# Attention's weighted sums in float32 column tiles, in a kernel of attention, experts and a dense block

## The chip, the cores and the metric

The kernel runs on one core of a Trainium2 chip. The metric is device time of one execution in microseconds (us), the median of several executions. Five engines work side by side, each through its own queue in order: TensorE (PE in the profile; its weight loads are PEld), VectorE (DVE), ScalarE (ACT), GpSimd (POOL) and SyncE (SP, which issues most DMAs). PSUM is the memory that TensorE writes its results to, in banks of 128 x 512 float32; SBUF is the working memory.

## The reference, cut to what matters

```
B, H, S, D = 2, 8, 768, 64        # 16 clusters
q_assign = argmax(q_n @ c_n.T);  k_assign = argmax(k_n @ c_n.T)
mask   = q_assign[:, None] == k_assign[None, :]
scores = where(mask, q @ k.T / 8, -1e9)
attn   = exp(scores - max(scores));  attn /= sum(attn) + 1e-9
x      = attn @ v                  # 16 heads of 768 x 64
x      = moe(x)                    # 1536 tokens, 8 experts, 512 -> 1024 -> 512, one expert a token
out    = gelu_like(x @ w_in) @ w_out   # 512 -> 2048 -> 512
```

All is float32. The route of a token hangs on an argmax, so the kernel works close to float32 precision throughout.

## The kernel before, in words

Attention runs first (to about 273 us), then the experts, then the dense block; the change touches attention alone.

A *unit* is a pair of heads of one batch: 8 units. A head has 6 query tiles of 128 rows, so a unit has 12 *steps* and the whole 96 (`steps`, L410). Three query tiles of a head are a *group*: 32 groups. The order of all work is written out by hand in the loop at L708, and each engine does its part in that order. One round i of the loop issues:

- `emit_scores(i + 1)` (L416): four matmuls of 384 columns into one of two score banks pairs (`sp`), in fp32r (a faster matmul form of rounded float32). Hi and lo parts of q and k are stacked in the contraction, and the one-hot rows of the clusters ride along in `Q2` and `Z`, so that the mask comes out of the matmul. VectorE takes the negative row maximum `nm` (L434).
- the output stage `ostage` (L481) of a group, in every third step: three matmuls with `wo` add the two 64-row halves of the weighted sum, transpose it back and append router logits; VectorE divides by the row sums (L489).
- `prepare(i)` (L686): pieces of the preparation of the next unit, by the table `plan_at` (L681). A piece can be: three transposes of q or k of one head (L255) into a bank, from which ScalarE casts H (L258) and VectorE the remainder L (L259); the DMAs that stack them (L273); the cluster scores (L330) and the argmax over 16 clusters; the one-hot rows (L342) and their eight DMAs (L348); the split of v into hi and lo, `vst` (L391).
- one third of a weighted sum, if one is queued (`part`, L464): four matmuls of a group's twelve.
- `emit_pt(i - 1)` (L442): six transposes of the probabilities, three to a bank. ScalarE copies each half into `pth` as fp32r (L452), VectorE subtracts it from the bank into `ptl` (L453).
- `emit_exp(i + 1)` (L436): ScalarE's exponential with row sums.

The weighted sum has `vst` (128 keys x [hi 64, lo 64]) as stationary and `pth`, then `ptl`, as moving operand, 384 queries wide: 6 key tiles x 2 = 12 matmuls of the full array. Rows 0 to 63 of the result are the sums with hi, rows 64 to 127 those with lo, and `wo` adds the two.

PSUM has `ps_s` (two score tiles of two banks), `ps_t` (two banks for transposed probabilities), `ps_a` (one bank for the weighted sum) and `ps_m` (one bank for all else: output stage, transposes of q and k, cluster scores, routing). `misc` (L228) hands out the bank of a preparation piece.

While the second batch is computed, the first one is routed: `route(0)` is advanced two small steps at each half of `emit_pt` (`advance`, L454), mostly on VectorE, with scalings on GpSimd (L598) and scatters (L603). The last three steps (`TAIL`) pop two parts of a weighted sum each. After the loop come the last weighted sums, the last routing, 90 small matmuls that keep TensorE busy (`keep_clock_last`) and the loads of the first expert.

Of the kernel before, what the change touches and what calls it, by code (L numbers as in the profile page):

```python
# [9 lines left out]
F32 = mybir.dt.float32  # L10
F32R = mybir.dt.float32r
BF16 = mybir.dt.bfloat16
I32 = mybir.dt.int32
AF = mybir.ActivationFunctionType
ALU = mybir.AluOpType
# [4 lines left out]
B, H, S, D = 2, 8, 768, 64  # L20
C = 16
# [4 lines left out]
T = S // 128  # L26
# [10 lines left out]
DATA_DEP = mybir.DependencyInfo(mybir.DependencyClass.Sync, mybir.DependencyReason.DATA)  # L37


def tile_t(j):  # L40

    return 2 * (j % 3) + j // 3
# [3 lines left out]
def attention_moe_ffn(ctx: ExitStack, tc: tile.TileContext, q, k, v, centroids, w_gate, w_og, w1, w2, w_in, w_out, out):  # L46
    nc = tc.nc
    const = ctx.enter_context(tc.tile_pool(name="const", reuse_waits="tile", bufs=1))

    def f32(ap):  # L50
        return ap.bitcast(F32)
# [4 lines left out]
    rev16 = const.tile([128, C], F32, name="rev16")  # L56
# [65 lines left out]
    def load_unit(u):  # L122
        b, pr = UNITS[u]
        d = st[u] = {}
        for nm, src in (("q", q), ("k", k), ("v", v)):
            t = ld.tile([128, 2, T, D], F32, name=f"ld_{nm}", tag=f"ld_{nm}")
            nc.sync.dma_start(out=t, in_=src[b, 2 * pr:2 * pr + 2].rearrange("h (p t) d -> p h t d", t=T))
            d[nm] = t

# [98 lines left out]
    def misc(u, nm):  # L228

        pool, tag = spots[0]  # L230
        if len(spots) > 1:
            spots.append(spots.pop(0))
        return pool.tile([128, 512], F32, name=nm, tag=tag)

    def prep_pieces(u):
        d = st[u]

        def alloc():
            for nm in ("Q1", "X"):
                d[nm] = stk.tile([128, 2, S], F32R, name=nm, tag=nm)  # L240
            for nm in ("Q2", "Z"):
                d[nm] = stk.tile([XW, 2, S], F32R, name=nm, tag=nm)
            for nm in ("Hq", "Lq", "Hk", "Lk"):
                d[nm] = one.tile([128, 2, 3 * 128], F32R, name=nm, tag=nm)
            d["sc"] = one.tile([128, 4, T, C], F32, name="sc", tag="sc")
            d["vst"] = stk.tile([128, 2, T, 2 * D], F32R, name="vst", tag="vst")

        def transposes(nm, h):
            def f():
# [41 lines left out]
            return f  # L291

        def argmax_a(x=slice(0, 4)):
            eng = nc.gpsimd if x == slice(0, 4) else nc.vector
            if "eq" not in d:
                d["m1"] = one.tile([128, 4, T], F32, name="m1", tag="m1")
                d["eq"] = one.tile([128, 4, T, C], F32, name="eq", tag="eq")
            sc, m1, eq = (d[nm][:, x].rearrange(p) for nm, p in (("sc", "p x t c -> p (x t) c"), ("m1", "p x t -> p (x t)"), ("eq", "p x t c -> p (x t) c")))
            n = m1.shape[1]
            nc.vector.tensor_reduce(m1, sc, op=ALU.max, axis=AX.X)  # L300
            if eng is nc.vector:
                eng.tensor_tensor(eq, sc, m1[:, :, None].to_broadcast([128, n, C]), op=ALU.is_equal)
            else:
                eng.tensor_tensor(eq, sc, m1[:, :, None].to_broadcast([128, n, C]), op=ALU.subtract)
                eng.tensor_scalar(eq, eq, 0.0, None, op0=ALU.is_equal)
            eng.tensor_tensor(eq, eq, rev16[:, None, :].to_broadcast([128, n, C]), op=ALU.mult)

        def argmax_b(x=slice(0, 4)):
            if "oh" not in d:
# [29 lines left out]

        def rows_of_ones():  # L340
            ot = one.tile([128, S], F32R, name="ohT", tag="ohT")[:, :384]
            nc.gpsimd.tensor_scalar(ot, d["oT"], oh_scale, oh_bias, op0=ALU.mult, op1=ALU.add)  # L342
            for h in range(2):
                for dst, g in (("Z", 2 + h), ("Q2", h)):
                    for par in range(2):
                        cs = slice(384 * par, 384 * par + 384)
                        src = slice(32 * g + C * par, 32 * g + C * par + C)
                        nc.sync.dma_start(out=f32(d[dst][64:80, h, cs]), in_=f32(ot[src]))  # L348
# [28 lines left out]
        def first_argmax(x0):  # L377
            def f():
                if x0 == 0:
                    argmax_b_pad()  # L380
                argmax_a(slice(x0, x0 + 2))
                argmax_b(slice(x0, x0 + 2))
            return f
# [3 lines left out]
            d["oh"] = one.tile([128, T + 1, 4, C], BF16, name="oh", tag="oh")  # L387
            nc.gpsimd.memset(d["oh"][:, 0], 0.0)

        def vsplit():  # L390
            hi = d["vst"][:, :, :, 0:D]  # L391
            x = nc.gpsimd.tensor_copy(hi, d["v"]).ins
            if u:
                tc.add_manual_dep(x, d["chosen"], DATA_DEP, reason="the choice of clusters goes first")
            nc.gpsimd.tensor_tensor(d["vst"][:, :, :, D:2 * D], d["v"], f32(hi), op=ALU.subtract)

        if u == 0:
            return [
                [transposes("q", 0)], [transposes("q", 1), stacks("q", (0,)), transposes("k", 0), transposes("k", 1), stacks("k"), stacks("q", (1,))],
                [clusters("q"), first_argmax(0), clusters("k"), first_argmax(2)], [first_onehots], [vsplit], [lambda: onehots((1,))],  # L400
            ]
        return [
            [transposes("q", 0)], [transposes("q", 1), stacks("q")], [transposes("k", 0)], [transposes("k", 1), stacks("k")],
            [], [scores, by_token, argmax_a], [argmax_b], [chosen], [by_cluster, rows_of_ones, vsplit],
        ]


# [8 lines left out]
    def emit_scores(i):  # L416
        u, h, j = steps[i]
        d = st[u]
        L = live[i] = {}
        if j % 3 == 0:  # L420
            L["sm"] = pp.tile([128, 3], F32, name="sm", tag="sm")
            L["pth"] = ptp.tile([128, T, 384], F32R, name="pth", tag="pth")
            L["ptl"] = ptp.tile([128, T, 384], F32R, name="ptl", tag="ptl")
        else:
            for nm in ("sm", "pth", "ptl"):
                L[nm] = live[i - 1][nm]
        sp = L["sp"] = ps_s.tile([128, 2, 512], F32, name="sp", tag="sp")
        cs = slice(j * 128, (j + 1) * 128)
        for n in range(2):
            ks = slice(384 * n, 384 * n + 384)  # L430
            nc.tensor.matmul(sp[:, n, :384], d["Q1"][:, h, cs], d["X"][:, h, ks], start=True, stop=False)  # L431
            nc.tensor.matmul(sp[:, n, :384], d["Q2"][:, h, cs], d["Z"][:, h, ks], start=False, stop=True)  # L432
        nm = L["nm"] = pp.tile([128, 1], F32, name="nm", tag="nm")
        nc.vector.tensor_reduce(nm, sp[:, :, :384], op=ALU.max, axis=AX.XY, negate=True)  # L434
# [7 lines left out]
    def emit_pt(i):  # L442
        L = live[i]
        j = steps[i][2]
        for n in range(2):
            pt = ps_t.tile([128, 512], F32, name="pt", tag="pt")
            for r in range(3):
                nc.tensor.transpose(pt[:, r * 128:(r + 1) * 128], L["P"][:, n, r * 128:(r + 1) * 128], ident)  # L448
            src = pt[:, :384].rearrange("p (r c) -> p r c", r=3)
            qs = slice(128 * (j % 3), 128 * (j % 3) + 128)  # L450
            hi = L["pth"][:, 3 * n:3 * n + 3, qs]
            nc.scalar.copy(hi, src)  # L452
            nc.vector.tensor_tensor(L["ptl"][:, 3 * n:3 * n + 3, qs], src, f32(hi), op=ALU.subtract)  # L453
            advance(2)  # L454

    av = deque()
# [2 lines left out]
    def queue_av(i):  # L459
# [1 line left out]
        L = live[i]  # L461
        hold = {}

        def part(m):  # L464
            def f():
                if m == 0:
                    hold["o"] = ps_a.tile([128, 512], F32, name="po", tag="po")
                for kt in range(2 * m, 2 * m + 2):
                    w = st[u]["vst"][:, h, tile_t(kt), :]
                    nc.tensor.matmul(hold["o"][:, :384], w, L["pth"][:, kt, :], start=(kt == 0), stop=False)  # L470
                    nc.tensor.matmul(hold["o"][:, :384], w, L["ptl"][:, kt, :], start=False, stop=(kt == T - 1))  # L471
                if m == 2:
                    oa = hold["oa"] = pp.tile([128, 384], F32, name="oa", tag="oa")
                    nc.scalar.copy(oa, hold["o"][:, :384])
                    rs = hold["rs"] = pp.tile([128, 3], F32, name="rs", tag="rs")
                    nc.vector.tensor_scalar(rs, L["sm"], 1e-9, None, op0=ALU.add)
                    nc.vector.reciprocal(rs, rs)
                    ost.append(ostage)
            return f

        def ostage():  # L481
            b, pr = UNITS[u]
# [7 lines left out]
            if (hh, j0) == (H - 1, 0) and b == B - 1:  # L490
                routing.append(route(1))

        av.extend([part(0), part(1), part(2)])


    rt = {}
# [182 lines left out]

    plan_at = {}  # L680
    for u in range(1, len(UNITS)):  # L681
        for n, r in enumerate((-3, -2, 0, 1, 3, 4, 6, 7, 8) if u > 1 else (0, 0, 0, 1, 3, 4, 6, 7, 8)):
            plan_at.setdefault((12 * (u - 1) + r, n == 6), []).append((u, n))
    pieces = {}

# [7 lines left out]
    with tc.manual_schedule():  # L693
# [14 lines left out]
        for i in range(NS + 2):  # L708
# [4 lines left out]
            if i + 1 < NS:  # L713
                emit_scores(i + 1)
            tail = i >= NS - TAIL
            if (tail or i % 3 == 2) and ost:
                ost.popleft()()
            prepare(i)
            if i == 0:
# [527 lines left out]
```

## Time and profile before

| | |
|---|---|
| median of 3 runs | 755.31 us (752.32 to 755.86) |
| the profiled execution | 755.41 us, of which the traced span is 753.6 |
| ScalarE busy | 422.3 us (56%) |
| GpSimd busy | 267.8 us (36%) |
| DMA, HBM over the span | 98.23 MB moved, 102 GB/s |

The busy time of an engine is an average over attention, experts and dense block, which have different limits; here attention is read by itself. Matmuls overlap, so a matmul's own duration is longer than the distance from its start to the next one's: in a timeline the distance of starts is what it costs.

### The profile page before, as it was taken

What the parts mean: (1) busy time and instruction counts of PE and PEld (TensorE: products, weight loads), DVE (VectorE), ACT (ScalarE), POOL (GpSimd) and SP (SyncE); (2) the same over time, 40 slices, a digit from 0 to 9 for tenths busy, and PEclk for the clock granted to TensorE, in tenths of its full rate; (3) what the DMA queues carried; (4) which work ended last, traced back from release to release, by engine and by line L of the source; (5) the groups of instructions that cost most, each with busy time, mean ns of one, the idle gap of its engine ahead of it and who ended that gap; (6) DMA issues with size and microseconds to landing.
All of it is one profiled execution on the core that took longest, in us unless ns stands there. A gap on an engine that the chain in (4) does not pass through costs nothing.

```text
span 753.6 us, 12278 instructions
## 1 busy us (share of the span) xinstructions
PE 721.8 (96%) x4314; PEld 635.2 (84%) x4314; DVE 509.5 (68%) x1000; ACT 422.3 (56%) x873; POOL 267.8 (36%) x205
## 2 busy tenths in 40 slices
PE   8999999999899978999999988999999999999996
PEld 5799899898799967999989888777888888888885
DVE  6899999999989982444776666797655556332322
ACT  3787787777778753456767776445434344212120
POOL 4112131120841023666768888232333122020202
PEclk7899999999999987999999999999999999999999
DMA  8756749438160037756756775133534311010101
GB/s 232 158 159 185 209 144 298 117 87 194 54 172 11 1 107 262 264 186 213 252 172 239 242 245 194 56 113 112 58 54 60 75 64 57 0 57 0 57 1 56
DMA packets 66241, 98.23 MB, mean 130 GB/s; under 512 B 9249, under 2 KB 44961, under 8 KB 66177
## 3 DMA queue, kind: packets, MB, share of 16 engines
q1 hardware_dynamic: 63872, 91.12, 42.4%
q0 software_dynamic: 2304, 6.30, 2.2%
q8 instruction: 35, 0.57, 0.3%
q14 instruction: 30, 0.24, 0.1%
HBM read 64.46 MB, written 12.59 MB: 102 GB/s over the span
## 4 chain that ended last, share of the span: by engine, by line
PE 57%; issue 16%; DVE 13%; ACT 5%; POOL 4%; DMA 4%; SPq 1%; POOLq 0%; ACTq 0%; DVEq 0%
PE pt L448 6%; PE po L470 4%; PE ph L1076 4%; PE ph L1075 4%; PE ph L1077 4%; PE sp L432 3%; PE po L471 3%; PE sp L431 3%; PE py L1169 3%; PE py L1168 3%; PE py L1167 3%; ACT w L799 2%; PE pox L487 2%; DVE ptl L453 2%; DVE nm L434 2%
## 5 line engine op out<-in xcount | busy, mean ns | idle before, releaser
L802 POOL TENSOR_TENSOR w<-raw,w 128x1024 fp32r<-128x1024 f32 x47 | 117.1, 2505 | 34.9 <-ACT w L799 19.3
L452 ACT CAST pth<-pt 128x384 fp32r<-128x384 f32 x192 | 83.7, 484 | 43.5 <-PE pt L448 43.4
L453 DVE TENSOR_TENSOR ptl<-pt,pth 128x384 fp32r<-128x384 f32 x192 | 97.6, 546 | 14.3 <-ACT pth L452 13.9
L1152 DVE TENSOR_TENSOR sg<-ph,sg 128x512 f32<-128x512 f32 x48 | 33.2, 691 | 103.5 <-ACT sg L1151 103.1
L434 DVE TENSOR_REDUCE nm<-sp 128x1 f32<-128x768 f32 x96 | 90.9, 947 | 4.3 <-PE sp L432 4.3
L849 POOL TENSOR_TENSOR w<-csq,w 128x512 fp32r<-128x512 f32 x32 | 43.5, 1359 | 139.0 <-ACT w L848 137.2
L440 ACT ACTIVATE P<-sp,nm 128x768 f32<-128x768 f32 x96 | 88.0, 917 | 3.0 <-DVE nm L434 2.8
L1151 ACT ACTIVATE sg<-ph 128x512 f32<-128x512 f32 x48 | 28.7, 598 | 108.7 <-PE ph L1077 105.4
L448 PE MATMUL pt<-ident,P 128*128 128x128 f32 x576 | 80.9, 274 | 2.4 <-DVE ptl L453 2.3
L448 PEld LDWEIGHTS pt<-ident,P 128*128 128x128 f32 x576 | 67.7, 141 | 10.4 <-DVE ptl L453 6.4
L1076 PE MATMUL ph<-ytl,w 128*128 128x512 f32 x192 | 76.1, 396 | 0.0
L1075 PE MATMUL ph<-yth,w 128*128 128x512 f32 x192 | 76.0, 396 | 0.0
L1077 PE MATMUL ph<-yth,w 128*128 128x512 f32 x192 | 75.6, 394 | 0.0
L1168 PE MATMUL py<-w,gh 128*128 128x512 f32 x192 | 75.3, 392 | 0.0
L1169 PE MATMUL py<-w,gl 128*128 128x512 f32 x192 | 75.2, 392 | 0.0
L1167 PE MATMUL py<-w,gh 128*128 128x512 f32 x192 | 75.0, 390 | 0.0
L431 PE MATMUL sp<-X,Q 128*128 128x384 f32 x192 | 73.9, 385 | 0.6 <-DMA X<-Lk 0.6
L799 ACT CAST w<-raw 128x1024 fp32r<-128x1024 f32 x64 | 66.8, 1044 | 6.3 <-DMA raw<-in_moe_w_dram 5.5
L470 PE MATMUL po<-pth,vst 128*128 128x384 f32 x192 | 70.3, 366 | 0.0
L899 PE MATMUL py<-ht,w 128*128 128x480 f32 (+5 forms) x192 | 61.0, 369 | 8.3 <-DVE room L906 5.1
L432 PE MATMUL sp<-Z,Q 80*128 80x384 f32 x192 | 66.5, 346 | 2.1 <-DMA Q<-ohT 2.1
L471 PE MATMUL po<-ptl,vst 128*128 128x384 f32 x192 | 64.9, 338 | 0.0
(240 smaller groups left out, 1676.0 us busy)
## 6 DMA issues: line engine op xcount, KB each, us to landing
raw<-in_moe_w_dram SPq DMA_DIRECT2D x64, 512.0 KB, 3.9
raw<-in_moe_w_in_dram SPq DMA_DIRECT2D x16, 512.0 KB, 4.2
raw<-in_moe_w_out_dram SPq DMA_DIRECT2D x16, 512.0 KB, 4.1
Q<-Hq SPq DMA_DIRECT2D x32, 192.0 KB, 6.0
xd<-zrow SPq DMA_DIRECT2D x8, 768.0 KB, 6.2
ld_q<-in_q_dram SPq DMA_DIRECT2D x8, 384.0 KB, 3.5
ld_k<-in_k_dram SPq DMA_DIRECT2D x8, 384.0 KB, 4.3
ld_v<-in_v_dram SPq DMA_DIRECT2D x8, 384.0 KB, 6.0
```

What stands on the lines that cost most here:

```text
L431: nc.tensor.matmul(sp[:, n, :384], d["Q1"][:, h, cs], d["X"][:, h, ks], start=True, stop=False)
L434: nc.vector.tensor_reduce(nm, sp[:, :, :384], op=ALU.max, axis=AX.XY, negate=True)
L448: nc.tensor.transpose(pt[:, r * 128:(r + 1) * 128], L["P"][:, n, r * 128:(r + 1) * 128], ident)
L453: nc.vector.tensor_tensor(L["ptl"][:, 3 * n:3 * n + 3, qs], src, f32(hi), op=ALU.subtract)
L470: nc.tensor.matmul(hold["o"][:, :384], w, L["pth"][:, kt, :], start=(kt == 0), stop=False)
L802: (eng or nc.gpsimd).tensor_tensor(lo, r, f32(hi), op=ALU.subtract)
L1075: nc.tensor.matmul(ph, wa(key, 0, k, i), yth[:, k, cs], start=(k == 0), stop=False)
L1076: nc.tensor.matmul(ph, wa(key, 0, k, i), ytl[:, k, cs], start=False, stop=False)
L1077: nc.tensor.matmul(ph, wa(key, 1, k, i), yth[:, k, cs], start=False, stop=(k == 3))
L1167: nc.tensor.matmul(po[m], gh[:, ms], wb(key, 0, i), start=first, stop=False)
L1168: nc.tensor.matmul(po[m], gh[:, ms], wb(key, 1, i), start=False, stop=False)
L1169: nc.tensor.matmul(po[m], gl[:, ms], wb(key, 0, i), start=False, stop=last)
```

## The change

- The probabilities are kept as one float32 tile `pT` instead of `pth` and `ptl`. Of each step's two halves ScalarE copies the first, VectorE the second.
- The weighted sum takes v as it was loaded (no split; `ld_v` gets four buffers instead of two) and multiplies in float32. The 64 columns of v go in two slices of 32; with the parity of the key tile that makes four column tiles of 32 columns, each writing 32 partitions of the same bank. All 12 matmuls of a group are issued in one step.
- After the first unit, transposes of q and k go to the bank of the weighted sum (`ps_a`) instead of `ps_m`.
- The argmax for units 1 to 7 moves from GpSimd (three passes) to VectorE (two), the scaling of the one-hot rows from GpSimd to ScalarE.
- The cluster scores move from a unit's step 4 to step 5, directly before a weighted sum, and the output stage from each third step (i % 3 == 2) to i % 3 == 0.

```diff
-            t = ld.tile([128, 2, T, D], F32, name=f"ld_{nm}", tag=f"ld_{nm}")
+            t = ld.tile([128, 2, T, D], F32, name=f"ld_{nm}", tag=f"ld_{nm}", bufs=4 if nm == "v" else 2)
...
+        elif nm == "pqk":
+            pool, tag = ps_a, "po"
...
-            if eng is nc.vector:
-                eng.tensor_tensor(eq, sc, m1[:, :, None].to_broadcast([128, n, C]), op=ALU.is_equal)
-            else:
-                eng.tensor_tensor(eq, sc, m1[:, :, None].to_broadcast([128, n, C]), op=ALU.subtract)
-                eng.tensor_scalar(eq, eq, 0.0, None, op0=ALU.is_equal)
-            eng.tensor_tensor(eq, eq, rev16[:, None, :].to_broadcast([128, n, C]), op=ALU.mult)
+            nc.vector.tensor_tensor(eq, sc, m1[:, :, None].to_broadcast([128, n, C]), op=ALU.is_equal)
+            nc.vector.tensor_tensor(eq, eq, rev16[:, None, :].to_broadcast([128, n, C]), op=ALU.mult)
...
-            nc.gpsimd.tensor_scalar(ot, d["oT"], oh_scale, oh_bias, op0=ALU.mult, op1=ALU.add)
+            nc.scalar.activation(ot, d["oT"], AF.Identity, scale=oh_scale, bias=oh_bias)
...
-            hi = L["pth"][:, 3 * n:3 * n + 3, qs]
-            nc.scalar.copy(hi, src)
-            nc.vector.tensor_tensor(L["ptl"][:, 3 * n:3 * n + 3, qs], src, f32(hi), op=ALU.subtract)
+            dst = L["pT"][:, 3 * n:3 * n + 3, qs]
+            if n == 0:
+                nc.scalar.copy(dst, src)
+            else:
+                nc.vector.tensor_copy(dst, src)
...
+        def weighted():
+            po = ps_a.tile([128, 512], F32, name="po", tag="po")
+            for kt in range(T):
+                for a in range(2):
+                    g = 2 * (kt % 2) + a
+                    nc.tensor.matmul(po[32 * g:32 * g + 32, :384], st[u]["v"][:, h, tile_t(kt), 32 * a:32 * a + 32],
+                                     L["pT"][:, kt, :], start=kt < 2, stop=kt >= T - 2)
...
-        av.extend([part(0), part(1), part(2)])
+        av.append(weighted)
...
-        for n, r in enumerate((-3, -2, 0, 1, 3, 4, 6, 7, 8) if u > 1 else (0, 0, 0, 1, 3, 4, 6, 7, 8)):
+        for n, r in enumerate((-3, -2, 0, 1, 3, 5, 6, 7, 8) if u > 1 else (0, 0, 0, 1, 3, 5, 6, 7, 8)):
...
-            if (tail or i % 3 == 2) and ost:
+            if (tail or i % 3 == 0) and ost:
```

The functions `vsplit` and `part` go with their calls; the copy out of the bank (`oa`) and the reciprocal row sums stay as they were.

## Rows read from the trace of the kernel before

**Rows 1.** The page, busy time of each engine, share of span, instructions.

```profile
PE 721.8 (96%) x4314; PEld 635.2 (84%) x4314; DVE 509.5 (68%) x1000; ACT 422.3 (56%) x873; POOL 267.8 (36%) x205
```

**Rows 2.** Busy time by stretch: its length, then engines, granted clock, DMA share, GB/s.

```profile
100.00:150.00 50.00, 49.46 (x351) 45.99 (x350) 47.49 (x96) 39.66 (x93) 9.59 (x9) 1.00 0.60 172
```

**Rows 3.** Timeline of TensorE, one group: start, duration, line, result<-operands, shape, count.

```profile
243.39 0.42 PE L431 MATMUL sp<-X,Q 128*128 128x384 f32 x1
...
244.19 0.79 PE L487 MATMUL pox<-wo,oa 128*128 128x80 f32 x6
244.77 0.42 PE L470 MATMUL po<-pth,vst 128*128 128x384 f32 x1
245.03 0.34 PE L471 MATMUL po<-ptl,vst 128*128 128x384 f32 x1
...
245.57 0.81 PE L448 MATMUL pt<-ident,P 128*128 128x128 f32 x6
246.14 0.42 PE L431 MATMUL sp<-X,Q 128*128 128x384 f32 x1
...
250.27 0.42 PE L431 MATMUL sp<-X,Q 128*128 128x384 f32 x1
```

**Rows 4.** Timeline of TensorE around one block of cluster scores.

```profile
153.45 0.33 PE L432 MATMUL sp<-Z,Q 80*128 80x384 f32 x1
153.72 0.52 PE L330 MATMUL pcl<-Hq,cfull 128*32 128x384 f32 x2
...
154.06 0.49 PE L330 MATMUL pcl<-Hq,cfull 128*32 128x384 f32 x2
...
154.39 0.49 PE L330 MATMUL pcl<-Lq,cfull 128*32 128x384 f32 x2
...
154.71 0.49 PE L330 MATMUL pcl<-Lq,cfull 128*32 128x384 f32 x2
...
155.15 0.44 PE L470 MATMUL po<-pth,vst 128*128 128x384 f32 x1
```

**Rows 5.** Groups by line, 60:250: count, busy us, mean ns, idle before, releaser.

```profile
L453 DVE TENSOR_TENSOR ptl<-pt,pth 128x384 fp32r<-128x384 f32 x146 | 74.1, 546 | 11.0 <-ACT pth L452 10.7
L434 DVE TENSOR_REDUCE nm<-sp 128x1 f32<-128x768 f32 x73 | 69.1, 947 | 1.0 <-PE sp L432 1.0
L440 ACT ACTIVATE P<-sp,nm 128x768 f32<-128x768 f32 x73 | 67.0, 918 | 0.5 <-DVE nm L434 0.3
L452 ACT CAST pth<-pt 128x384 fp32r<-128x384 f32 x146 | 63.4, 484 | 33.6 <-PE pt L448 33.6
...
L259 DVE SCALAR_TENSOR_TENSOR Lq<-pqk,Hq 128x384 fp32r<-128x384 f32 x10 | 5.4, 540 | 0.0
```

**Rows 6.** Timeline of TensorE, starts of three steps with q transposes.

```profile
166.15 0.42 PE L431 MATMUL sp<-X,Q 128*128 128x384 f32 x1
...
168.55 0.42 PE L431 MATMUL sp<-X,Q 128*128 128x384 f32 x1
...
171.16 0.42 PE L431 MATMUL sp<-X,Q 128*128 128x384 f32 x1
```

**Rows 7.** Timeline of TensorE, starts of the same step in three units.

```profile
63.36 0.42 PE L431 MATMUL sp<-X,Q 128*128 128x384 f32 x1
...
94.06 0.42 PE L431 MATMUL sp<-X,Q 128*128 128x384 f32 x1
...
222.00 0.42 PE L431 MATMUL sp<-X,Q 128*128 128x384 f32 x1
```

**Rows 8.** Waits of TensorE, 24:273: us in total, times, longest.

```profile
PE pt L448 <- DVE ptl L453: 2.3, 8, 0.5
PE sp L432 <- DMA Q<-ohT: 2.1, 2, 1.8
```

**Rows 9.** Timeline of TensorE at the end of attention.

```profile
262.84 0.42 PE L431 MATMUL sp<-X,Q 128*128 128x384 f32 x1
...
273.51 0.34 PE L471 MATMUL po<-ptl,vst 128*128 128x384 f32 x1
```

More of the change, by code (lines that the diff above doesn't have):

```diff
@@ L245, in alloc @@
             d["sc"] = one.tile([128, 4, T, C], F32, name="sc", tag="sc")
-            d["vst"] = stk.tile([128, 2, T, 2 * D], F32R, name="vst", tag="vst")
         def transposes(nm, h):
@@ L293, in argmax_a @@
         def argmax_a(x=slice(0, 4)):
-            eng = nc.gpsimd if x == slice(0, 4) else nc.vector
             if "eq" not in d:
@@ L388, in argmax_b_pad @@
             nc.gpsimd.memset(d["oh"][:, 0], 0.0)
[L390 to L395, printed above, removed]
         if u == 0:
@@ L399, in prep_pieces @@
                 [transposes("q", 0)], [transposes("q", 1), stacks("q", (0,)), transposes("k", 0), transposes("k", 1), stacks("k"), stacks("q", (1,))],
-                [clusters("q"), first_argmax(0), clusters("k"), first_argmax(2)], [first_onehots], [vsplit], [lambda: onehots((1,))],
+                [clusters("q"), first_argmax(0), clusters("k"), first_argmax(2)], [first_onehots], [lambda: onehots((1,))],
             ]
@@ L403, in prep_pieces @@
             [transposes("q", 0)], [transposes("q", 1), stacks("q")], [transposes("k", 0)], [transposes("k", 1), stacks("k")],
-            [], [scores, by_token, argmax_a], [argmax_b], [chosen], [by_cluster, rows_of_ones, vsplit],
+            [], [scores, by_token, argmax_a], [argmax_b], [chosen], [by_cluster, rows_of_ones],
         ]
@@ L421, in emit_scores @@
             L["sm"] = pp.tile([128, 3], F32, name="sm", tag="sm")
-            L["pth"] = ptp.tile([128, T, 384], F32R, name="pth", tag="pth")
-            L["ptl"] = ptp.tile([128, T, 384], F32R, name="ptl", tag="ptl")
+            L["pT"] = ptp.tile([128, T, 384], F32, name="pT", tag="pT")
         else:
-            for nm in ("sm", "pth", "ptl"):
+            for nm in ("sm", "pT"):
                 L[nm] = live[i - 1][nm]
@@ L462, in queue_av @@
         hold = {}
[L464 to L479, printed above, removed]
+        def weighted():
[5 more added lines that the diff above has]
+                                     L["pT"][:, kt, :], start=kt < 2, stop=kt >= T - 2)
+            oa = hold["oa"] = pp.tile([128, 384], F32, name="oa", tag="oa")
+            nc.scalar.copy(oa, po[:, :384])
+            rs = hold["rs"] = pp.tile([128, 3], F32, name="rs", tag="rs")
+            nc.vector.tensor_scalar(rs, L["sm"], 1e-9, None, op0=ALU.add)
+            nc.vector.reciprocal(rs, rs)
+            ost.append(ostage)
         def ostage():
```

## The prediction, made before the changed kernel ran

> **What bounds the kernel now.** I read the busy times first, then stretches of the attention part, then TensorE's instructions in order of time, then who waits for whom. TensorE is busy for 96% of the span [rows 1]. That alone proves little, so the attention part (about 24 to 273 us) has to be read by itself. Between 100 and 150 us TensorE has 49.5 of 50 us, VectorE 47.5, ScalarE 39.7, at the full granted clock of 1.00 (2.4 GHz) [rows 2]. So TensorE is the bound and VectorE stands right behind it.
>
> The timeline of one group of three query tiles shows the bound instruction by instruction [rows 3]. The group starts at 243.39 and the next at 250.27: 6.88 us. Inside it everything is back to back: four score matmuls take 0.80, the output stage (L487) 0.58, then four matmuls of the weighted sum, then six transposes 0.57 (245.57 to 246.14). Weighted-sum matmuls follow each other every 0.18 us (245.03 to 245.57 is three), and the first one after another kind takes 0.26. Of the 6.88 us, 12 x 0.175 + 0.09 = 2.19 are the weighted sum. There is no gap to fill: whatever lightens VectorE and ScalarE gains nothing in such a group. The time must come from TensorE's own work or from groups that are not like this one.
>
> **1. The weighted sum itself.** It removes 12 matmuls (full array, 2.19 us a group) and adds 12 float32 matmuls of 32 columns, each in one of four column tiles. The kernel before has this very form: the cluster scores (L330), four column tiles, 128x384 float32, two matmuls deep [rows 4]. Each float32 matmul is two passes; four tiles run a pass together, and such rounds start at 153.72, 154.06, 154.39, 154.71: 0.34, then 0.33. Eight matmuls are four rounds, so twelve are six: 0.34 + 5 x 0.325 = 1.96. Going in costs 0.09 (153.45 to 153.72 is 0.27 instead of 0.18), coming out 0.11 (154.71 to 155.15 is 0.44 instead of 0.33). The first instruction afterwards may lose another 0.10, as full-array matmuls do after a change of kind. So 2.16 to 2.26 against 2.19: -0.03 to +0.07 a group, for 32 groups -1 to +2. I take +0.5. Twice the precision in the moving operand costs TensorE nothing here, because four tiles share the array.
>
> The Trainium skill (TensorEngine Tiling, Tiling Modes, Key Properties) says that changing the tiling mode drains TensorE, which speaks against 32 small tiled blocks between full-array ones. The trace agrees, at 0.09 in and 0.11 out; the sum above is already made with it.
>
> In seven units the cluster scores move one step on, to stand directly before a weighted sum, so one way in and out goes. A group with scores now costs 6.88 + 4 rounds (1.31) instead of 6.88 + 0.09 + 1.43 + 0.11: -0.32 each, -2.2 together (bounds -2.5 and 0).
>
> **2. Transposes of q and k.** There are 28 blocks of three. A step with the first of a pair takes 2.40 instead of 2.07 (166.15 to 168.55), the second 2.61 [rows 6]. Now no weighted sum follows them, but transposes of the same kind: the 0.09 of a change of kind goes, 28 x 0.09 = -2.5. They move into the one bank of the weighted sum, which adds a wait. The weighted sum in the next step cannot start before ScalarE (H) and VectorE (L) have emptied that bank. ScalarE, counted from the first half's transposes of the step before, still does a copy, an exponential and the cast: 0.48 + 0.92 + 0.48; then VectorE's L, 0.54 [rows 5]: 2.42. TensorE has 0.28 + 0.80 + 0.25 + 0.57 + 0.80 = 2.70 of work until then, but ScalarE and VectorE each lose some tenths to handovers and to the first block's H and L. The wait is between 0 and one L (0.54). I take half, 0.27, for 14 pairs: +3.8 (0 to +7.6). Behind it TensorE's transposes queue, and nothing else can pass. Net of this part: +1.3 (bounds -2.5 and +5).
>
> **3. Splits that go, and what they hid.** Per half tile ScalarE copied (0.48) and VectorE subtracted (0.55) [rows 5], one after the other; now the first half is one ScalarE copy and the second one VectorE copy, side by side. Per step VectorE falls from 0.95 + 2 x 0.55 = 2.05 to about 0.95 + 0.5 (a copy is not shown: 0.4 to 0.55, the longer end being the nearest row), ScalarE from 0.92 + 2 x 0.48 to 0.92 + 0.48. GpSimd loses the v split and the argmax; two VectorE passes of 128x384 (at most 2 x 0.6 a unit) and one ScalarE cast (about 0.5 a unit) take its place. These are hidden by the room just made: about 0.6 a step, 7 us a unit of 12 steps. Without that cover they would cost 7 x 1.7 = 12. In a calm group all this is worth nothing.
>
> Where it pays is in the uneven stretches. A calm unit takes 30.70 us (63.36 to 94.06); the five units from 63.36 to 222.00 take 158.64, that is 5.1 more than five calm ones [rows 7]. TensorE's waits there and at both ends are for the one-hot rows' DMA (2.1 us) and for VectorE's subtraction (2.3 us in 8 waits) [rows 8]. The one-hot rows were made on GpSimd, in the queue where the first batch's routing scales its rows; on ScalarE they come earlier. VectorE's backlog (sums of logits, small routing steps) meets a VectorE with a quarter of its time free. I expect most of the 5.1 and about 1 more from the first steps and the last unit to go: -5.2 (bounds -2 and -7). The next thing late there is the bank wait of part 2.
>
> **4. The end of attention.** From the last score matmuls (262.84) to the last matmul of the last weighted sum (273.51 + 0.18) it takes 10.85 us [rows 9]; here TensorE waits for the chain, not the other way. New chain: scores 0.80, weighted sum 2.16, ScalarE's copy out, half copy and exponential 0.48 + 0.48 + 0.92, transposes 0.57, a half copied 0.48, weighted sum 2.16: 8.05. Five handovers between engines come on top; the trace has waits of up to 0.5 for one [rows 8], I take 0.2 each. That is 9.05, so -1.8 (bounds -0.5 and -2.5, the latter if routing's VectorE steps stay out of the way). Everything behind it (scatter, expert weights, MoE, dense) only shifts; its loads queue on SP behind the scattered rows as before, so I cost them at nothing.
>
> **Sum.** +0.5 - 2.2 + 1.3 - 5.2 - 1.8 = -7.4. The profiled execution took 755.4 us (span 753.6, 1.8 around it), 0.1 from the median of 755.3. Forecast 748.0.
>
> **Rivals.**
> A. The waits only change their name. TensorE stays full in calm groups, the bank wait of part 2 is at 0.45 a pair, VectorE's new passes and the copies keep the first batch's routing late. For it: the loop through one bank and ScalarE's strict order (the exponential stands behind two copies). Against it: VectorE's room. Parts: +1, -1.5, +3.8, -3.5, -1.5: -1.7, 753.7.
> B. Slower: the rounds of the weighted sum do not overlap as those of the cluster scores do. Here two tiles stream the same probabilities, and v is read as 32-column slices of its rows; the scores had four different streams. If a round lasts as long as one pass is shown (0.49) [rows 4], 192 rounds cost 192 x 0.16 = +31: 779. It decides from 0.04 more a round (+7.4). Against it: the passes of L330 also add to one place in every round, and start 0.01 apart.
> The Trainium skill (TensorE: Matmul & The Clock Gate, Part 3) gives 2.38 times for three column tiles, not three. By that a round would be 0.325 / 0.79 = 0.41, an estimate, and the time about 764. The trace has four tiles in 0.325 each round and does not bear it out.
> C. More: no bank wait, all uneven stretches calm, no loss at leaving tiles. The favourable ends: -1 - 2.5 - 2.5 - 7 - 2.5 = -15.5, 740.
>
> **How the numbers follow.** Forecast 0.55 (its own range 744 to 752), A 0.22, B 0.08, C 0.15. The bounds of all parts reach from 740 to 761; I give 741 to 756, which leaves out the end of C and B. A measurement of this kernel tells about 0.5% from no change, 3.8 us: faster means under 751.5. Faster: 0.51 of the forecast, C, and 0.04 of A: 0.70. Slower: B and a little of A: 0.09. The rest, 0.21, is within.
>
> **What will show it.** In the changed timeline a calm group should take 6.8 to 6.95 us, with six rounds 0.32 to 0.34 apart in one step of three; that tests part 1, and rounds over 0.36 show B. Groups with q and k transposes: a wait of TensorE's weighted sum for L (VectorE) of 0.1 to 0.4, 14 times, tests part 2; none is C, over 0.45 is A. Units of 30.3 to 30.7 throughout and no wait for the one-hot rows' DMA test part 3; VectorE should fall to about 37 of 50 us with TensorE still at 49. From the last scores to the last weighted sum about 9 us tests part 4. I am wrong if the group length of TensorE moves by more than 0.2, or if a stage behind attention changes its length.

## The result, and the profile after

The changed kernel takes 743.9 us (median of 6 runs, 742.41 to 745.99), the kernel before 754.33 (6 runs, 752.32 to 755.86). The ratio is 0.9866, 95% interval 0.9844 to 0.9888: 10.4 us less. The forecast was 748.0 with 741 to 756 around it. The profiled execution of the changed kernel took 743.06 us, span 741.4; before it was 755.41 and 753.6.

The busy times of the page of the changed kernel answer to [rows 1]; the row of the stretch from 100 to 150 us (same columns) to [rows 2].

```profile
PE 715.3 (96%) x4698; PEld 587.8 (79%) x4698; DVE 476.1 (64%) x918; ACT 391.6 (53%) x784; POOL 221.4 (30%) x161
```

```profile
100.00:150.00 50.00, 49.42 (x431) 37.32 (x424) 39.95 (x77) 33.73 (x75) 0.00 (x0) 1.00 0.65 178
```

TensorE is as full as before (49.42 of 50, was 49.46), at the same granted clock of 1.00 (2.4 GHz). VectorE fell from 47.49 to 39.95, ScalarE from 39.66 to 33.73. As the prediction said, that alone moves nothing in a calm group: this is TensorE's timeline of one, which answers to [rows 3].

```profile
227.87 0.44 PE L419 MATMUL sp<-X,Q 128*128 128x384 f32 x1
...
228.33 0.34 PE L419 MATMUL sp<-X,Q 128*128 128x384 f32 x1
228.50 0.33 PE L420 MATMUL sp<-Z,Q 80*128 80x384 f32 x1
228.76 2.14 PE L459 MATMUL po<-pT,ld_v 128*32 128x384 f32 x24
230.84 0.88 PE L436 MATMUL pt<-ident,P 128*128 128x128 f32 x6
231.47 0.42 PE L419 MATMUL sp<-X,Q 128*128 128x384 f32 x1
...
232.27 0.79 PE L474 MATMUL pox<-wo,oa 128*128 128x80 f32 x6
232.89 0.82 PE L436 MATMUL pt<-ident,P 128*128 128x128 f32 x6
233.47 0.42 PE L419 MATMUL sp<-X,Q 128*128 128x384 f32 x1
...
234.85 0.44 PE L419 MATMUL sp<-X,Q 128*128 128x384 f32 x1
```

The group takes 6.98 us (227.87 to 234.85); before 6.88. The 12 float32 matmuls stand in the trace as 24 passes (x24); the block of them costs 2.08 here (228.76 to 230.84), 2.07 in most groups. The transposes behind it cost 0.63 instead of 0.58 (230.84 to 231.47, against 232.89 to 233.47).

A group with a pair of q transposes, from the same timeline earlier on:

```profile
40.18 0.42 PE L419 MATMUL sp<-X,Q 128*128 128x384 f32 x1
...
41.59 0.49 PE L256 MATMUL pqk<-ident,ld_q 128*128 128x128 f32 x3
...
43.28 0.52 PE L256 MATMUL pqk<-ident,ld_q 128*128 128x128 f32 x3
...
45.09 2.14 PE L459 MATMUL po<-pT,ld_v 128*32 128x384 f32 x24
...
47.80 0.42 PE L419 MATMUL sp<-X,Q 128*128 128x384 f32 x1
```

The weighted sum at 45.09 starts as close to its scores (0.87 from their start at 44.22) as in the calm group (0.89): TensorE does not wait for the bank. VectorE empties it just in time, at 45.00:

```profile
44.45 0.55 DVE L260 SCALAR_TENSOR_TENSOR Lq<-pqk,Hq 128x384 fp32r<-128x384 f32 x1
```

The two transposes cost 0.33 (41.59 to 41.92) and 0.36 (43.28 to 43.64), so the group is 7.62: 0.64 over the calm one.

The same step in several units answers to [rows 7] (58.81 begins the step with the cluster scores), and the end of attention to [rows 9]:

```profile
57.43 0.42 PE L419 MATMUL sp<-X,Q 128*128 128x384 f32 x1
58.81 0.44 PE L419 MATMUL sp<-X,Q 128*128 128x384 f32 x1
...
59.71 0.52 PE L326 MATMUL pcl<-Hq,cfull 128*32 128x384 f32 x2
...
61.03 2.12 PE L459 MATMUL po<-pT,ld_v 128*32 128x384 f32 x24
...
63.71 0.42 PE L419 MATMUL sp<-X,Q 128*128 128x384 f32 x1
...
87.94 0.42 PE L419 MATMUL sp<-X,Q 128*128 128x384 f32 x1
...
217.51 0.42 PE L419 MATMUL sp<-X,Q 128*128 128x384 f32 x1
...
254.42 0.42 PE L419 MATMUL sp<-X,Q 128*128 128x384 f32 x1
...
262.27 0.83 PE L459 MATMUL po<-pT,ld_v 128*32 128x384 f32 x8
```

A calm unit takes 30.51 (57.43 to 87.94), was 30.70. The five units of the stretch with the first batch's routing take 153.80 (63.71 to 217.51), were 158.64. From the last scores to the start of the last weighted-sum matmul (262.27 + 0.83 - 0.49 = 262.61) it is 8.19, was 10.67.

In the kernel before the step with the cluster scores began at 59.67 and ended at the 63.36 of [rows 7]:

```profile
59.67 0.42 PE L431 MATMUL sp<-X,Q 128*128 128x384 f32 x1
```

TensorE's waits, 24 to 270 us (total, times, longest), answer to [rows 8]; two more of 0.2 each are left out. The waits for `ptl` and for the one-hot rows' DMA are gone. The wait for `roh` is the last routing, at 266.5, behind the last weighted sum; before it had the same 1.94 there, at 277.25. The largest within attention is for `oa`.

```profile
PE prk L535 <- DVE roh L516: 1.9, 1, 1.9
PE pox L474 <- ACT oa L462: 1.2, 2, 0.6
PE pnt L617 <- DVE dest L550: 0.5, 1, 0.5
```

### The profile page after: what moved, and what is told of

It is laid out like the page before. It is cut to its first block, busy times and chain, and to the rows that moved or that the text cites. A ratio compares the mean times of both kernels' runs of the same rounds, so it can differ in the third digit from the quotient of the medians.

```text
span 741.4 us, 12821 instructions
## 1 busy us (share of the span) xinstructions
PE 715.3 (96%) x4698; PEld 587.8 (79%) x4698; DVE 476.1 (64%) x918; ACT 391.6 (53%) x784; POOL 221.4 (30%) x161
## 4 chain that ended last, share of the span: by engine, by line
PE 27%; issue 16%; DVE 9%; ACT 5%; POOL 3%; DMA 2%; POOLq 0%; SPq 0%; ACTq 0%; DVEq 0%
PE ph L1064 3%; PE ph L1063 3%; PE ph L1062 3%; PE py L1156 3%; PE py L1155 3%; PE py L1154 3%; ACT w L786 2%; DMA xr<-xd 2%; DVE w L789 1%; PE py L886 1%; PE ph L886 1%; DVE ct L824 1%; DVE ph L893 1%; POOL out_dram L1164 1%; PE py L884 1%
## 5 line engine op out<-in xcount | busy, mean ns | idle before, releaser
L436 PEld LDWEIGHTS pt<-ident,P 128*128 128x128 f32 x576 | 65.1, 143 | 21.3 <-issue 19.4
L443 DVE COPY pT<-pt 128x384 f32<-128x384 f32 x96 | 52.8, 550 | 27.5 <-PE pt L436 27.1
L459 PE MATMUL po<-pT,ld_v 128*32 128x384 f32 x768 | 68.4, 489 | 0.2 <-ACT pT L441 0.2
L886 PE MATMUL ph<-t,w 128*128 128x480 f32 (+5 forms) x192 | 61.1, 370 | 1.5 <-DVE ht L910 1.5
L585 POOL TENSOR_SCALAR xs<-xw,gate 128x512 f32<-128x512 f32 x6 | 9.9, 1643 | 174.6 <-DVE gate L567 174.2
```

The costliest lines, as they stand in the source:

```text
L886: nc.tensor.matmul(ps[:, :2 * n], w_hi, t, start=first, stop=False)
```

## Experiments

Medians below are each kernel's own; ratios are against the kernel before on the same chip, where its median was 754.44 to 754.50 (754.33 with the result). "The changed kernel" is 743.9 us.

### What a round of column tiles costs

**Twice the rounds.** Each group's sum is made twice over into the same bank (the second time starts afresh, so the sums stay as they were).

```diff
-            for kt in range(T):
+            for kt in list(range(T)) * 2:
```

> The changed kernel with every weighted sum computed twice over in the same block (the second pass starts afresh, so the result stays). It measures the price of a round without the way in and out. My theory: six more rounds of 0.325 in each of 32 groups, +1.95 a group, +62 us, as nothing but TensorE bounds these steps. Rival: a good part of the 2.07 us is the way in and out or a wait; then the block grows by clearly less than 1.95.

805.63 us, ratio 1.067 (1.0634 to 1.0707), 61.7 more than the changed kernel. TensorE's timeline:

```profile
79.79 4.08 PE L459 MATMUL po<-pT,ld_v 128*32 128x384 f32 x48
...
83.80 0.87 PE L436 MATMUL pt<-ident,P 128*128 128x128 f32 x6
```

The block takes 4.01 (79.79 to 83.80) instead of 2.07: six rounds cost 1.94, 0.323 each. 32 x 1.94 = 62.1, which is all of the 61.7. So the rounds are priced as the prediction read them from the cluster scores [rows 4], and the whole price lies on the path.

**Two tiles of 64 columns instead of four of 32**: half the matmuls, as many rounds.

```diff
-                for a in range(2):
-                    g = 2 * (kt % 2) + a
-                    nc.tensor.matmul(po[32 * g:32 * g + 32, :384], st[u]["v"][:, h, tile_t(kt), 32 * a:32 * a + 32],
-                                     L["pT"][:, kt, :], start=kt < 2, stop=kt >= T - 2)
+                g = kt % 2
+                nc.tensor.matmul(po[64 * g:64 * g + 64, :384], st[u]["v"][:, h, tile_t(kt), :],
+                                 L["pT"][:, kt, :], start=kt < 2, stop=kt >= T - 2)
```

> The changed kernel with two column tiles of 64 columns (6 matmuls a group) in place of four of 32 (12 matmuls). My theory: what counts is rounds of one pass through the array, 0.325 us each, and both forms need six (12 matmuls x 2 passes / 4, or 6 x 2 / 2), so the weighted sum stays at 2.07 and the time within 1 us. Rival: the number of concurrent tiles sets the gain (four hide more than two), then a weighted sum takes over 3 us and the time rises by 30 us or more.

746.55 us, ratio 0.9894 (0.9868 to 0.992): 2.6 more, outside what was expected.

```profile
61.67 0.52 PE L326 MATMUL pcl<-Hq,cfull 128*32 128x384 f32 x2
...
63.10 2.16 PE L458 MATMUL po<-pT,ld_v 128*64 128x384 f32 x12
65.19 0.87 PE L436 MATMUL pt<-ident,P 128*128 128x128 f32 x6
```

The block is nearly the same: 2.09 (63.10 to 65.19). What grew is its neighbour: the cluster scores stay four tiles of 32 and now stand beside a block of two tiles of 64. In this kernel's timeline they cost 1.43 (61.67 to 63.10) instead of 1.32 (59.71 to 61.03 in the changed kernel), and a calm unit 30.69 instead of 30.51. 7 x 0.18 = 1.3 of the 2.6; the rest is not assigned.

**One tile of 64 columns**: every pass by itself (the output stage then contracts over 64 rows).

```diff
-                for a in range(2):
-                    g = 2 * (kt % 2) + a
...
+                nc.tensor.matmul(po[0:64, :384], st[u]["v"][:, h, tile_t(kt), :],
+                                 L["pT"][:, kt, :], start=kt == 0, stop=kt == T - 1)
...
-            nc.scalar.copy(oa, po[:, :384])
+            nc.scalar.copy(oa[0:64], po[0:64, :384])
...
-                nc.tensor.matmul(pv[:, r], hold["oa"][:, r * 128:(r + 1) * 128], wo[:, hh], start=True, stop=True)
+                nc.tensor.matmul(pv[:, r], hold["oa"][0:64, r * 128:(r + 1) * 128], wo[0:64, hh], start=True, stop=True)
```

> The changed kernel with the float32 weighted sum in one column tile of 64 columns: 6 matmuls one after the other, twelve rounds in place of six. It shows what running tiles side by side is worth. My theory: 12 x 0.325 = 3.9 us a group, +1.85 to +2.0, +59 to +64 us in all. Rival: the block is bound by something else than rounds (reading the probabilities), and it stays under 3 us.

816.92 us, ratio 1.0823 (1.0801 to 1.0844), 73 more.

```profile
121.38 4.08 PE L457 MATMUL po<-pT,ld_v 128*64 128x384 f32 x12
125.40 0.88 PE L436 MATMUL pt<-ident,P 128*128 128x128 f32 x6
```

The block takes 4.02 (121.38 to 125.40): 1.95 more, 62 us over 32 groups, as expected of the block. The time is over the 59 to 64 that were expected. Of the other 11 the expectation did not count the output stage: in its 64-row form it takes 0.82 (126.91 to 127.73 in this timeline) instead of 0.62, 6 us in all. The rest is not assigned. Two tiles side by side are thus worth 4.02 / 2.09 = 1.92, close to two.

### The bank and the neighbours

**q and k transposes back in `ps_m`.**

```diff
-        elif nm == "pqk":
-            pool, tag = ps_a, "po"
```

> The changed kernel with the transposes of q and k back in the bank that the output stage uses, not that of the weighted sum. My theory: the first transposes of each pair then follow the output stage directly and wait for VectorE to empty its bank (about 0.6 us, 14 times), so groups with q and k take 8.0 to 8.3 us instead of 7.6 and the time rises by 5 to 9 us. Rival: with one wait less in front of the weighted sum it is equal or better, 7.4 to 7.6 us a group, time -2 to +1.

756.24 us, ratio 1.0028 (1.0011 to 1.0044): 12.3 more, the whole gain, and more than the 5 to 9 that were expected. TensorE's timeline, and the row of the waits:

```profile
74.70 0.79 PE L472 MATMUL pox<-wo,oa 128*128 128x80 f32 x6
...
76.30 0.55 PE L254 MATMUL pqk<-ident,ld_q 128*128 128x128 f32 x3 [0.81 <-DVE xw L474]
```

```profile
PEld pqk L254 <- DVE xw L474: 10.2, 11, 1.3
```

The output stage now stands in the same step as the transposes. In one bank they take turns, and VectorE's division (`xw`) is what the transposes wait for. A group with transposes is about 1.0 longer (8.66 and 8.60 against 7.62); 14 pairs make 14, a little over the 12.3. So the move to the weighted sum's bank is no loss to be accepted, as the prediction had it, but what makes the new order possible. The old place of the output stage with the old bank was not run.

**Cluster scores back at step 4**, away from the weighted sum.

```diff
-        for n, r in enumerate((-3, -2, 0, 1, 3, 5, 6, 7, 8) if u > 1 else (0, 0, 0, 1, 3, 5, 6, 7, 8)):
+        for n, r in enumerate((-3, -2, 0, 1, 3, 4, 6, 7, 8) if u > 1 else (0, 0, 0, 1, 3, 4, 6, 7, 8)):
```

> The changed kernel with the cluster scores back in step 4 of a unit, away from the weighted sum. My theory: the way into and out of the column tiles is paid twice, 0.3 us in each of 7 units: a calm unit takes 30.8 us instead of 30.5 and the time rises by 2 us (1.5 to 3). Rival: changing the tiling costs nothing and the scores may stand anywhere: unit 30.5, time within 0.5 us.

747.25 us, ratio 0.9907 (0.9883 to 0.9931): 3.35 more. Its calm unit is 30.77, the changed kernel's 30.51: 0.26 a unit, 1.8 over seven. One change of tile form saved is worth that; the other 1.5 is not assigned (the six runs of this kernel spread over 1.7 us, those of the changed kernel over 3.6).

### GpSimd, VectorE and the room on it

**The kernel before without GpSimd in the preparation**: argmax on VectorE, one-hot scaling on ScalarE, nothing else changed.

```diff
-            eng = nc.gpsimd if x == slice(0, 4) else nc.vector
+            eng = nc.vector
...
-            nc.gpsimd.tensor_scalar(ot, d["oT"], oh_scale, oh_bias, op0=ALU.mult, op1=ALU.add)
+            nc.scalar.activation(ot, d["oT"], AF.Identity, scale=oh_scale, bias=oh_bias)
```

> The kernel before with one part of the change: the argmax of units 1 to 7 on VectorE (two passes) and the one-hot scaling on ScalarE; the split of v and the 24 weighted-sum matmuls of a pair of groups stay. My theory: GpSimd's part in the gain is the one-hot rows' late DMA (2.1 us) and a little port trouble, and VectorE, at 47.5 of 50 us, gets 1.2 us more a unit, so the time moves by -3 to +4 us and the start (third step's scores at 23.9 us) stays as before. Rival: leaving GpSimd is the gain by itself; then -6 to -10 us.

763.04 us, ratio 1.0116 (1.009 to 1.0142): 8.7 slower. Both expectations missed. Two rows of its waits, 24 to 270 us:

```profile
ACT ohT L342 <- DVE oT L338: 14.2, 6, 3.1
...
PE pt L448 <- DVE ptl L453: 8.6, 12, 1.2
```

**Of the two, only the one-hot scaling** to ScalarE (the second edit of the diff above).

> The kernel before with the scaling of the one-hot rows on ScalarE and nothing else. My theory: the waits for the one-hot rows' DMA (2.1 us of TensorE's) go, as the scaling no longer queues behind the routing on GpSimd, and nothing else changes: -1.5 to -2.5 us. Rival: ScalarE's strict order delays copies and exponentials behind it, as VectorE is late with the transposed one-hot rows: 0 or slower.

760.01 us, ratio 1.0069 (1.0051 to 1.0088): 5.5 slower, as the rival had it. The wait for the one-hot DMA is gone, yet the kernel lost time: the two waits of the run before stand here at 14.1 and 7.7 us. One instruction of ScalarE's timeline:

```profile
75.46 0.71 ACT L342 ACTIVATE ohT<-oT,oh_bias,oh_scale 128x384 fp32r<-128x384 bf16 x1 [2.04 <-DVE oT L338]
```

ScalarE works in order. The cast waits 2.04 us for VectorE's transpose `oT`, which is late because VectorE has no room. Behind the cast stand ScalarE's copies of the probabilities, behind them VectorE's subtractions, behind these TensorE. On GpSimd no copy of the probabilities stood behind it. So the move is a loss by itself in the kernel before.

**The changed kernel with argmax and one-hot scaling back on GpSimd.**

```diff
+            if x != slice(0, 4):
...
+                return
+            nc.gpsimd.tensor_tensor(eq, sc, m1[:, :, None].to_broadcast([128, n, C]), op=ALU.subtract)
+            nc.gpsimd.tensor_scalar(eq, eq, 0.0, None, op0=ALU.is_equal)
+            nc.gpsimd.tensor_tensor(eq, eq, rev16[:, None, :].to_broadcast([128, n, C]), op=ALU.mult)
...
-            nc.scalar.activation(ot, d["oT"], AF.Identity, scale=oh_scale, bias=oh_bias)
+            nc.gpsimd.tensor_scalar(ot, d["oT"], oh_scale, oh_bias, op0=ALU.mult, op1=ALU.add)
```

> The changed kernel with the argmax of units 1 to 7 and the one-hot scaling back on GpSimd. My theory: VectorE has room for these passes now, and GpSimd's own (3 us and 0.67 us) still end in time in a calm unit, where the table gives them whole steps; only while the first batch is routed does the one-hot DMA come late again. So +1 to +3 us, in one or two units. Rival: leaving GpSimd is what made the units even: then +4 to +6 us, spread over all units.

758.69 us, ratio 1.0049 (1.0031 to 1.0066): 14.8 more than the changed kernel, far over every expectation. Timelines of GpSimd, VectorE and TensorE in one unit:

```profile
66.36 0.84 POOL L305 TENSOR_TENSOR eq<-sc,m 128x384 f32<-128x384 f32 x1 [22.39 <-DVE rs L469]
...
68.55 1.00 POOL L307 TENSOR_TENSOR eq<-eq,rev 128x384 f32<-128x384 f32 x1
...
69.58 0.55 DVE L314 TENSOR_REDUCE m<-eq 128x24 f32<-128x384 f32 x1 [1.27 <-POOL eq L307]
...
71.83 0.55 PE L441 MATMUL pt<-ident,P 128*128 128x128 f32 x3 [1.08 <-DVE pT L448]
```

With the scores at step 5, three GpSimd passes (66.36 to 69.55) must be done before the second half of the argmax, one step later. VectorE stands 1.27 us for them, with its copies of the probabilities behind, and TensorE 1.08 for those, in every unit. TensorE's waits, 24 to 275 us, have 8.1 of the 14.8 in these seven, and 2.7 in one wait for the one-hot rows:

```profile
PE pt L441 <- DVE pT L448: 8.1, 7, 1.5
PE sp L425 <- DMA Q<-ohT: 2.7, 1, 2.7
```

**The same with the scores back at step 4** (both edits together).

> The changed kernel with argmax and one-hot scaling on GpSimd as in the run before, and the cluster scores back in step 4. My theory now: the run with GpSimd lost 15 us because the table leaves one step between scores (5) and the second half of the argmax (6), and VectorE's queue stands still until GpSimd's three passes are through; with two steps between them it should come to 747 to 751 us, and the 1.87 us blocks of transposes go. Rival: GpSimd's passes are slow for the kernel wherever they stand: 756 us or more.

749.23 us, ratio 0.9927 (0.9907 to 0.9946), as expected. The stall is gone; one wait for the one-hot rows is back:

```profile
PE sp L425 <- DMA Q<-ohT: 1.9, 1, 1.9
```

This kernel is the change without the moves off GpSimd and without the new place of the scores: 5.2 us under the kernel before. Moving both off GpSimd gives 2.0 more (to 747.25, the kernel with the scores at step 4; the intervals of the two ratios overlap, so this is little clear of scatter), and the place of the scores 3.35 more (to 743.9).

**Both halves of the probabilities copied by VectorE.**

```diff
-            if n == 0:
-                nc.scalar.copy(dst, src)
-            else:
-                nc.vector.tensor_copy(dst, src)
+            nc.vector.tensor_copy(dst, src)
```

> The changed kernel with both halves of the probabilities copied by VectorE (0.55 us each), ScalarE none. My theory: the change could take GpSimd's passes on VectorE, and got rid of the waits, because VectorE fell from 28.7 to 24.9 us in a unit of 30.5; 12 more copies of 0.5 make it 31, so VectorE becomes the bound in most units, a unit takes 31 to 32 us and the time rises by 4 to 12 us. Rival: TensorE's work alone sets the time and VectorE's load does not matter: within 1 us.

761.05 us, ratio 1.0079 (1.0052 to 1.0106): 17.2 more, over the 4 to 12 that were expected. VectorE is then nearly as full as before, TensorE no longer is (the row answers to [rows 2]), and a calm unit takes 32.3.

```profile
100.00:150.00 50.00, 48.16 (x403) 34.26 (x402) 46.48 (x94) 24.77 (x52) 0.00 (x0) 1.00 0.53 156
```

So the change needs the freed VectorE time: without it even the calm units grow, and more than the whole gain is lost. The run also puts the two copies of a step one behind the other on VectorE, and does not tell the load from that order.

### What is left, and the start

**The sum of router logits three steps earlier.** One step of the routing unit of the changed kernel is long: the output stage waits for ScalarE's copy `oa`, which stands behind the one-hot cast. ScalarE's and TensorE's timelines:

```profile
132.10 0.71 ACT L338 ACTIVATE ohT<-oT,oh_bias,oh_scale 128x384 fp32r<-128x384 bf16 x1 [2.33 <-DVE rs L464]
...
133.23 0.45 PE L474 MATMUL pox<-wo,oa 128*128 128x80 f32 x2 [0.57 <-ACT oa L462]
```

```diff
-            if i % (NS // 2) == NS // 2 - 5 and i < NS:
+            if i % (NS // 2) == NS // 2 - 8 and i < NS:
```

> The changed kernel with the sums of logits (1.13 us on VectorE) three steps earlier, where VectorE has no piece of preparation. My theory: the longest wait that is left in the middle of attention (a score step of 1.53 instead of 0.80 at 131.7 us, the output stage waiting for ScalarE's copy, which stands behind the one-hot scaling, which stands behind VectorE) goes: -0.8 us, hardly measurable in the time, plain in the timeline. Rival: it is not the sum that makes VectorE late there; the step stays over 1.3.

In its timeline the step's output stage follows its scores at 0.79 again (133.04 to 133.83). The unit went from 31.35 to 30.66, but the time is 744.31 (ratio 0.987, 0.985 to 0.989): 0.7 us can't be told from the scatter of these medians.

**The kernel before with the first unit's v split held back** until the clusters are chosen, to test whether GpSimd's split delays the start.

```diff
-            if u:
+            if True:
```

> The kernel before, with GpSimd's split of v for the first unit held back until the first unit's clusters are chosen. My theory: in the kernel before this split runs beside VectorE's argmax, slows it (is_equal 1.12 us beside it, 0.42 alone), the first scores come 1.2 us later and TensorE's granted clock stays at 0.50 (1.2 GHz) until about 23 us instead of 17. So the third step's scores should start at about 21.2 us instead of 23.9, the clock be 1.00 from about 18 us, and the time fall by 2.5 us. Rival: the earlier start of the changed kernel came from input DMAs that happened to land earlier; then the start stays at 23 to 24 us and the time within 1 us.

754.98 us, ratio 1.0006 (0.9989 to 1.0023): no change, as the rival had it. The scores of the third step start at 22.68 here, at 23.94 in the profile of before and at 21.20 in that of the changed kernel (first line before, second line changed):

```profile
23.94 0.42 PE L431 MATMUL sp<-X,Q 128*128 128x384 f32 x1
```

```profile
21.20 0.44 PE L419 MATMUL sp<-X,Q 128*128 128x384 f32 x1 [0.37 <-ACT P L428]
```

The granted clock differs there: it stands at 0.50 (1.2 GHz) from 11 to 23 us in the profile of before, and is back at 0.95 from 17 us in that of the changed kernel, where TensorE was busy for all of 15 to 17 us (in that of before for 0.84 of these 2 us); in the profile of this run it is 1.00 from 17 to 19 us and 0.50 again from 21 to 23.

Over all the profiles this start lies between 22.7 and 24.0 in kernels of the old form and between 21.2 and 24.1 in those of the new. The two compared profiles happen to stand near opposite ends: 2.7 of the 12.3 us between their profiled executions are at the start, and most of that looks like scatter, which fits the medians' smaller difference of 10.4.

## Why the prediction was right, and where its terms were not

The direction, the size (-10.4 against -7.4, inside the range) and the grounds were right: TensorE stays the bound, four tiles share the array, and the rest comes from uneven stretches. The terms one by one:

**1. The weighted sum: mechanism right, size off.** Predicted +0.5 (bounds -1 to +2). The group moved from 6.88 to 6.98: +0.10, 32 times, is +3.2, above the upper bound; the group was to stay within 6.95. The six rounds and the way in and out are as priced: the block's 2.08 and 0.09 before it make 2.17 (228.50, the last score matmul, to 228.76 is 0.26 instead of 0.17), predicted 2.16. What was under-counted is the transposes behind the block (0.05 more, every time) and the output stage that is now followed by another kind (0.62, was 0.58). The prediction allowed up to 0.10 for "the first instruction afterwards", took the middle of its bounds, and had nothing for the output stage.

The cluster scores beside the sum: predicted -2.2. Their step took 3.69 (59.67 to 63.36) where a plain one took 2.07, 1.62 for the scores; now it takes 4.90 (58.81 to 63.71) where one with a weighted sum takes 3.60 (227.87 to 231.47), 1.30. That is -0.32 a unit, -2.2 in seven. The term came out although its working adds the 0.11 of the way out to a 1.43 that holds it already: by its own rows it is -0.21 a unit. The measured 1.62 has another 0.1 that these rows do not show. Against the scores at step 4 in the changed kernel, a third order, the calm unit gives -1.8.

The Trainium skill (TensorEngine Tiling, Tiling Modes, Key Properties) says that a change of tiling mode drains TensorE. The runs agree: the cluster scores lost 0.11 next to tiles of another size (1.43 against 1.32), and the transposes 0.05 behind the block (0.63 against 0.58).

**Rival B (the rounds do not overlap) is out.** Doubling gives 0.323 a round, one tile instead of two nearly twice the time. The Trainium skill (TensorE: Matmul & The Clock Gate, Part 3) has 2.38 for three column tiles; three were not run here, but two gave 1.92, and four in a round cost what two cost (2.07 against 2.09).

**2. Transposes of q and k: two terms that did not come, and a missed reason.** Predicted -2.5 for a change of kind that goes, +3.8 for a wait at the shared bank. Neither came. The transposes take 0.33 and 0.36, not 0.25, and the weighted sum never waits. What the pairs gave follows from the calm unit: it moved by -0.19, of which four groups are +0.40 and the scores -0.32, so two pairs are -0.27, and 14 pairs -1.9 (predicted +1.3). Most of it is the second block of a q pair: its step was 0.54 over a plain one (2.61 against 2.07 [rows 6]), now it is 0.36; the first was 0.33 and still is. The step that failed is "The wait is between 0 and one L (0.54). I take half". The prediction's own sum, 2.42 for ScalarE and VectorE against 2.70 for TensorE, gave no wait; what it set on top for handovers and the first block had no size from a row. In the trace L is done at 45.00 and the weighted sum starts at 45.09, so nothing is waited for, though the margin is small. And it asked what the shared bank costs, not what the old bank would cost in the new order: 12.3 us.

**3. Uneven stretches: sum about right, reason partly wrong.** Predicted -5.2 (with the first steps and the last unit). The five units fell by 4.84, of which 5 x 0.19 belong to the calm unit, so -3.9. The one-hot wait and the `ptl` waits went, as said. But "on ScalarE they come earlier" does not pay by itself: in the kernel before the same move ends the wait too and costs 5.5. What the runs show is VectorE's room: with it the moves off GpSimd give about 2.0, without it they cost 5.5 (the scaling alone) and 8.7 (both), and taking it back alone costs 17.2. The prediction named 12 us as the price of the moved passes without cover; in the kernel before, which has no such room, it is 8.7. It had the room at "a quarter" of VectorE's time and VectorE at about 37 of 50 us; it is a fifth, 39.95.

**4. The end of attention.** Predicted -1.8, measured -2.5 (10.67 to 8.19 between starts): at the far end of its bounds.

**The sum.** +3.2 - 2.2 - 1.9 - 3.9 - 2.5 = -7.3 from rows of the two profiles. That this is so near the forecast's -7.4 is luck: part 1 came out 2.7 worse and part 2 3.2 better than predicted.

The other 3 of the 10.4 are not assigned. The two profiles, whose spans differ by 12.2, show where to look. Up to the third step's scores they differ by 2.7, from there to the last scores by 5.7 (23.94 to 262.84 against 21.20 to 254.42), at the end of attention by 2.5, from there to the experts by 0.8, and behind that by 0.5. So attention between these points gained 0.9 more than the terms have. The start varies by over 1 us either way between executions. From the last weighted sum to the first expert matmul it is 19.75 here and 20.55 before, and 19.4 to 20.3 in other profiles, so the difference can't be told from scatter. A real part that no run isolated may hide in both.

No run has the float32 weighted sum without the new order around it.

**Rival A** (waits change their name) fell with the bank wait, but its pattern showed in one place: the output stage that waits for `oa` behind a late one-hot cast. **Rival C** was about as near in time as the forecast (740 and 748 against 743.9): no bank wait and mostly calm units (30.5, 30.5, 31.4, 30.8 and 30.6 in the five), though not its cheaper groups.

## What to carry to other kernels

A bound engine that is full in calm stretches still gains from room on its neighbours, in the uneven stretches, but the room has to come first: here moving work to an engine that runs in order was a loss while what it waits for was late, because everything behind it waited too. Before costing what a shared bank adds, ask what the old bank would cost in the new order. Small matmuls of one tile form belong next to each other; each border between forms cost about a tenth of a microsecond on both sides here.

## What the runs showed of the hardware

- A round of float32 passes over 384 columns costs the same whether it holds two tiles of 64 columns or four of 32 (2.09 and 2.07 for six rounds; 0.323 for one more); one tile alone takes as long per pass (4.02 for twelve).
- Borders between tile forms cost also where both sides are column tiles: scores in four tiles of 32 took 1.32 beside their own form and 1.43 beside two tiles of 64.
- VectorE was slowed by GpSimd. The same pass took 1.12 us in the kernel before, beside GpSimd's split of v, and 0.38 in the changed kernel without it (timelines of before, GpSimd and VectorE, then of the changed kernel):

```profile
9.74 1.81 POOL L395 TENSOR_TENSOR vst<-ld_v,vst 128x768 fp32r<-128x768 f32 x1
...
10.64 1.12 DVE L302 TENSOR_TENSOR eq<-sc,m 128x192 f32<-128x192 f32 x1
```

```profile
10.78 0.38 DVE L301 TENSOR_TENSOR eq<-sc,m 128x192 f32<-128x192 f32 x1
```

The Trainium skill (SBUF — State Buffer, SBUF: two separate sides) says that a VectorE instruction with two SBUF inputs and a GpSimd instruction that reads SBUF exclude each other on a shared port; these rows agree. VectorE's pass ends at 11.76, 0.21 us after GpSimd's (11.55). In the profile with only the one-hot scaling moved, where it starts later, it takes 0.62 (from 11.28) and again ends 0.22 after GpSimd's (9.87 and 1.81); with the split held back it takes 0.36. It cost nothing here: with the split out of the way the time stayed the same (0.9989 to 1.0023).
